# One ring of eight PSUM banks, decoding by masks, and a first pooling on TensorE, in a kernel ordered by a planner

## The chip, the core and the metric

The program runs on one core of a Trainium2 chip. The metric is the device time of one execution in microseconds (us); lower is better. TensorE multiplies, VectorE, ScalarE and GpSimd work element by element, SyncE issues the transfers, and PSUM is the memory into which TensorE writes (eight banks of 128 partitions x 512 fp32). In the profile the engines are PE (PEld for its weight loads), DVE, ACT, POOL and SP.

## What is computed

Three layers follow one another. An attention over eight batches of eight heads, 576 tokens and 64 channels, whose keys and values are first averaged over groups of eight tokens; then a mixture of four causal attention experts, of which the gate takes two for each token; then a layer that mixes tokens and channels with cosine and sine.

```python
def _attn_ref(q, k, v):                      # q, k, v: (8, 8, 576, 64)
    k_p = k.reshape(B, H, 72, 8, D).mean(axis=3)
    v_p = v.reshape(B, H, 72, 8, D).mean(axis=3)
    attn = softmax(q @ k_p.transpose(0, 1, 3, 2) / sqrt(D))
    return attn @ v_p

def _moe_ref(x, w_gate, wq, wk, wv, wo):     # x: (8, 576, 512), 4 experts of 64 channels, 2 taken
    ...
    a = softmax(causal(x @ wq[e] @ (x @ wk[e]).T / sqrt(64)))
    ye = a @ (x @ wv[e]) @ wo[e]
    ...

def _moe2_ref(x, w_theta, w_tok_r, w_tok_i, w_ch):
    theta = x @ w_theta
    y = w_tok_r @ (x * cos(theta)) + w_tok_i @ (x * sin(theta))
    u = x + y
    return u + maximum(u @ w_ch, 0)
```

Some weights of the third layer (w_theta, w_tok, w_ch) come as 64-bit numbers and are turned into fp32 on the chip: this is the decoding.

## The kernel before

**Precision.** Nearly every product is made of three: each factor is held as a high half, rounded to the engine's short fp32 format, and a low half, the rest (`mm3`, line 481). The usual way out of PSUM is thus a pair: ScalarE copies (and so rounds) the product into the high half, VectorE subtracts that half from the product and writes the low one.

**Two halves.** The first half makes attention and experts. For each batch `pool_kv` (line 713) averages keys and values by adding, on GpSimd (for the first batch partly on VectorE, `FIRST_DVE`, line 28). ScalarE copies the pooled keys into `kbd`, the values into `vbd`; each is a block matrix whose zero half was cleared at the start, so both are written by halves of 64 partitions. `attn_half` (line 754) makes scores for tiles of 128 queries; `WHOLE` (line 26) says for which tiles the exponentials are made in one instruction (VectorE subtracts the maximum and sums) and for which in eight, one for each head with its own sum (ScalarE). It then transposes the scores (`pm`, `pq`) and multiplies by the values. `proj_qk` (815) and `proj_v` (847) make the experts' queries, keys, values and gates; the keys (`kh`) are copied to the other half of the partitions by a transfer. `scores`, `norm`, `turn` and `heads` (902 to 962) do the experts' attention. Attention of batch b+1 is interleaved with the experts of batch b, and `decode` (672) runs in four blocks for each of the first six batches; its results go to DRAM (`thD`, `tokD`) and are read back for the second half. The second half is `mix` (1105: angles, sine, cosine, times x) and `tokens` (1155: the two big products and the output).

**Banks.** Products of the projections, values, experts' outputs and the second half's big products take one of two banks called `acc`, transposes one of two called `t`, scores and the mixing's products one of four called `s`.

**Order.** The order of instructions on each engine is written out before the kernel is built. `Plan` (197) collects every instruction with what it depends on. `part` and `arrange` (332, 341) give each a key, a wished-for time: the start of its part in `PARTS` (43), spread over the part's length, plus a `SHIFT` (58) for its engine and the tensor that it writes. `issue` (361) then runs a list of engines with estimated durations (`price`, 305) and takes, at each step, the instruction that can start first, ties by key. Line 466 is where all instructions are issued, so every row of the profile names that line; tensors tell them apart.

Of the kernel before, what the change touches and what calls it, by code (L numbers as in the profile page):

```python
# [25 lines left out]
WHOLE = {1, 2, 3, 4}, {0}  # L26

FIRST_DVE = {"k0", "k2", "pm0", "v0", "vr", "vrb0", "w0", "w3", "w4", "w6"}
# [15 lines left out]
    "first": (-1302.83, 63.19), "kv first": (-249.24, 366.9), "attn first 0": (-2208.92, 30.55),  # L44
    "attn first 1": (-552.72, 6.54), "proj_v first 0": (-1145.19, 56.03), "proj_qk0 first 0": (-185.37, 1302.94),
# [3 lines left out]
    "moe1": (29.54, 22.32), "decode": (150.23, 0.58), "wp": (-141.08, 3.51), "loadc first": (-6.04, 1083.14),  # L49
    "wtok first": (-212.16, 3987.86), "moe1 last": (27.48, 103.73), "mix first": (770.4, 161.1),  # L50
    "wtok": (2281.89, 4299.31), "wch": (-794.95, 122.81), "loadc": (-901.73, 22508671.56), "tokens": (85.02, 33.36),
    "mix": (85.18, 31.94), "constants first": (-1492.94, 5143.97), "clear first": (-2169.17, 8594480.35),
    "weights first": (-1120.91, 244.57), "load 1": (-21.92, 2656.27), "load first k": (-1565.62, 16.63),
    "load first q": (-1211.16, 0.84), "load first v": (-1596.57, 239.37),
}
SHIFT = {
    "ACT.G": 310.7, "ACT.G*": -60.8, "ACT.chs": 547.28, "ACT.d_hi": 469.68, "ACT.d_raw": -47.45, "ACT.d_s": 807.39,
    "ACT.gates": 299.94, "ACT.gates*": 299.58, "ACT.kbd": -11.49, "ACT.kbd*": -340.09, "ACT.kh": -2.28,
    "ACT.kh*": 65.35, "ACT.pa": -42.54, "ACT.pa*": 44.32, "ACT.pev": 4.6, "ACT.pev*": -912.36, "ACT.pod": -26.03,
    "ACT.pod*": 798.55, "ACT.pp": 2.9, "ACT.pp*": -1318.06, "ACT.pr": -176.41, "ACT.pr*": -24.35, "ACT.pt": -169.18,  # L60
    "ACT.pt*": -352.19, "ACT.qs": -10.6, "ACT.qs*": -463.58, "ACT.r": -71.52, "ACT.r*": 9.14, "ACT.th": 625.3,
    "ACT.th*": -370.35, "ACT.us": 161.03, "ACT.v": -127.44, "ACT.v*": 190.03, "ACT.vbd": -58.15, "ACT.vbd*": -1060.98,
    "ACT.vrh": 239.89, "ACT.vrh*": 411.06, "ACT.wT": 282.39, "ACT.warm": -205.54, "ACT.wos": -220.19,
    "ACT.wps": -74.18, "ACT.wqs*": -160.07, "ACT.wvs*": -767.36, "ACT.x": -165.21, "ACT.x*": -338.71,
    "ACT.xT": -426.63, "ACT.xT*": -238.01, "ACT.xt": 269.77, "ACT.xt*": -447.57, "ACT.yg": -290.43, "ACT.yg*": -78.87,
    "ACT.ys": -37.1, "ACT.ys*": 255.73, "ACT.yst": -83.9, "ACT.yst*": 34.37, "ACT.z": 76.22, "ACT.z*": -67.57,
    "ACT.zt": -607.59, "ACT.zt*": -849.31, "CTL.": 608.37, "DMA.": -426.39, "DMA.d_raw": 513.05, "DMA.kh": 303.04,
    "DMA.kh*": 585.01, "DMA.kraw": 171.92, "DMA.kraw*": 98.53, "DMA.pev*": 255.52, "DMA.pm*": 185.77,
    "DMA.pod*": -63.81, "DMA.qraw": -231.98, "DMA.qraw*": -71.33, "DMA.thD": 250.39, "DMA.ths": 592.41,
    "DMA.tokD": 134.39, "DMA.toks": -521.25, "DMA.toks*": -394.74, "DMA.v": -569.25, "DMA.v*": 95.2,  # L70
    "DMA.vraw": 149.85, "DMA.vraw*": -103.2, "DMA.vrem": 318.96, "DMA.vrem*": 108.24, "DMA.x": 69.1,
    "DMA.ygD": -74.78, "DMA.ygD*": -418.7, "DMA.yraw": 159.13, "DMA.yraw*": -144.65, "DMA.ytail": -390.7,
    "DMA.ytail*": 114.16, "DMA.zf": 736.52, "DVE.before*": 163.28, "DVE.cmp": -602.52, "DVE.cmp*": -395.89,
    "DVE.d_raw": 67.78, "DVE.flush": 65.65, "DVE.gates*": -533.48, "DVE.hm*": 633.13, "DVE.hpi": 704.94,
    "DVE.ident": -188.3, "DVE.kl": -3.31, "DVE.kl*": -148.18, "DVE.kt*": -647.74, "DVE.l": -309.76, "DVE.l*": 24.84,
    "DVE.lb": -7.23, "DVE.lb*": -163.3, "DVE.limit*": 210.65, "DVE.logit": 221.32, "DVE.logit*": 367.23,
    "DVE.m": -56.69, "DVE.m*": -115.98, "DVE.mask*": 659.33, "DVE.mx": 144.89, "DVE.mx*": 334.45, "DVE.o": -41.03,
# [14 lines left out]
    "POOL.vbd*": -610.85, "POOL.vrb": -61.96, "POOL.vrb*": 327.56, "POOL.vrl": -106.84, "POOL.vt": -45.14,  # L92
    "POOL.vt*": 491.07, "POOL.wT": 171.13, "POOL.wos": 289.44, "POOL.wqs*": -1583.79, "POOL.wvs*": 204.79,
    "POOL.yraw": 435.28, "POOL.yraw*": 343.16, "POOL.ys": -841.0, "POOL.ys*": -50.81, "POOL.yst": 441.93,
    "POOL.yst*": -91.42, "POOL.ytail": 463.31, "POOL.ytail*": 436.57, "POOL.z": 255.2, "POOL.z*": -199.85,
}


# [1164 lines left out]
```

## Time and profile before

| | us |
|---|---|
| median of 3 runs (980.51 to 984.83) | 982.76 |
| the profiled execution's own time | 980.56 |
| its span, first to last instruction | 978.8 |
| TensorE busy | 916.0 (94%) |
| ScalarE busy | 650.3 (66%) |
| VectorE busy | 600.0 (61%) |
| GpSimd busy | 516.7 (53%) |

The 1.8 us between span and time lie around the program. The shares are means over two very different halves, so they are read by stretches of the span. A product's busy time runs until it has drained, some 0.28 us for one that takes 0.12 us in a row of others, so a busy TensorE isn't one at its peak.

### The profile page before, as it was taken

Reading aid. Unit: us, or ns where it says so; the run is one execution under the profiler, and the core shown is the slowest. Engines: PE = TensorE matmul, PEld = TensorE weight load, DVE = VectorE, ACT = ScalarE, POOL = GpSimd, SP = SyncE. Lnnn points to the kernel's source line nnn. Section 1 sums busy time; section 2 is a strip of 40 time slices with the busy share of each in tenths; the row PEclk is TensorE's granted clock in tenths of the full one; section 3 lists DMA queues with packets and bytes.
Section 4 is the critical chain, followed back from the end, with each engine's and each line's share of the span. In section 5 each row is a group of like instructions: output and inputs, shape, how many; then the busy total and the mean of one; then the engine's idle time right before and its main releaser. Section 6 shows DMA issues by size and latency. Waiting matters only on the chain.

```text
span 978.8 us, 19095 instructions
## 1 busy us (share of the span) xinstructions
PE 916.0 (94%) x6384; PEld 858.5 (88%) x6384; DVE 600.0 (61%) x1718; ACT 650.3 (66%) x2026; POOL 516.7 (53%) x693
## 2 busy tenths in 40 slices
PE   2888999999899999999888999999999999999998
PEld 2887988898889899988866799999999999999998
DVE  5877887787878788887756745272424534262412
ACT  4689989798888999987768864262535444363510
POOL 7877777577386755544355774261625335151420
PEclk9999999999999999999989999999999999999999
DMA  9444445335444433334277413020110202010001
GB/s 279 138 143 122 122 123 150 115 108 140 119 118 116 136 96 87 89 103 115 51 232 243 154 44 92 1 85 13 38 56 13 80 1 70 1 38 13 25 25 49
DMA packets 78434, 91.63 MB, mean 94 GB/s; under 512 B 11264, under 2 KB 60928, under 8 KB 78336
## 3 DMA queue, kind: packets, MB, share of 16 engines
q1 hardware_dynamic: 78336, 90.41, 31.4%
q8 instruction: 51, 0.84, 0.4%
q14 instruction: 47, 0.39, 0.1%
HBM read 58.34 MB, written 26.28 MB: 86 GB/s over the span
## 4 chain that ended last, share of the span: by engine, by line
PE 64%; ACT 17%; DVE 8%; DMA 4%; POOL 3%; issue 3%; SPq 1%; POOLq 0%; ACTq 0%; DVEq 0%
PE acc L466 46%; PE s L466 14%; PE t L466 4%; ACT pp L466 4%; ACT pt L466 2%; DMA kh<-kh 2%; ACT pev L466 2%; ACT qs L466 1%; DVE s L466 1%; ACT kh L466 1%; ACT pa L466 1%; DVE pa L466 1%; DMA qraw<-in_qT_dram 1%; ACT xT L466 1%; DVE kl L466 1%
## 5 line engine op out<-in xcount | busy, mean ns | idle before, releaser
L466 PE MATMUL acc<-toks,z 128*128 128x288 f32 x1536 | 242.3, 297 | 2.0 <-ACT z L466 1.0
L466 PEld LDWEIGHTS acc<-toks,z 128*128 128x128 f32 x1536 | 223.9, 188 | 9.5 <-POOL z L466 1.8
L466 POOL TENSOR_TENSOR us<-u,us 128x288 fp32r<-128x288 f32 x64 | 51.9, 811 | 198.4 <-ACT us L466 198.3
L466 PE MATMUL acc<-xT,wqs 128*128 128x256 f32 (+1 forms) x768 | 123.3, 303 | 3.4 <-DVE logit L466 1.4
L466 PE MATMUL acc<-us,chs 128*128 128x288 f32 x768 | 114.1, 297 | 0.6 <-DVE o L466 0.5
L466 PEld LDWEIGHTS acc<-xT,wqs 128*128 128x128 f32 x768 | 106.4, 189 | 7.5 <-PE acc L466 3.4
L466 PEld LDWEIGHTS acc<-us,chs 128*128 128x128 f32 x768 | 107.9, 188 | 5.0 <-DVE o L466 1.5
L466 DVE TENSOR_TENSOR u<-acc,xt 128x288 f32<-128x288 f32 x64 | 29.1, 455 | 132.4 <-PE acc L466 132.4
L466 ACT CAST us<-u 128x288 fp32r<-128x288 f32 x64 | 27.6, 431 | 120.6 <-DVE u L466 120.5
L466 POOL TENSOR_TENSOR z<-zf,z 128x512 fp32r<-128x512 f32 x64 | 81.9, 1298 | 33.7 <-ACT z L466 33.6
L466 POOL TENSOR_SCALAR pev<-pev,lb,G 128x128 f32<-128x128 f32 (+4 forms) x80 | 52.5, 657 | 72.6 <-DVE lb L466 30.0
L466 DVE TENSOR_TENSOR pt<-t,pt 128x512 fp32r<-128x512 f32 (+4 forms) x160 | 75.7, 484 | 15.2 <-ACT pt L466 13.2
L466 ACT ACTIVATE pp<-s,mx 128x72 f32<-128x72 f32 x232 | 74.6, 336 | 6.6 <-DVE mx L466 6.0
L466 PE MATMUL acc<-wvs,xT 128*128 128x260 f32 x480 | 77.6, 292 | 1.2 <-DVE kl L466 0.4
L466 DVE CUSTOM_DVE_ANT_0 s<-s,mask 128x128 f32<-128x128 f32 (+2 forms) x144 | 69.6, 494 | 14.7 <-PE s L466 12.7
L466 ACT CAST pt<-t 128x512 fp32r<-128x512 f32 (+4 forms) x160 | 67.8, 437 | 13.8 <-PE t L466 12.9
L466 PE MATMUL s<-kbd,qraw 128*128 128x144 f32 x320 | 60.3, 311 | 16.2 <-DMA qraw<-in_qT_dram 12.3
L466 PE MATMUL acc<-pt,v 128*128 128x320 f32 (+4 forms) x416 | 68.1, 296 | 5.6 <-ACT yg L466 1.6
L466 PE MATMUL s<-kh,qs 128*128 128x128 f32 (+2 forms) x192 | 62.3, 355 | 10.3 <-DMA kh<-kh 8.0
L466 PEld LDWEIGHTS acc<-pt,v 128*128 128x128 f32 x416 | 60.7, 191 | 11.2 <-ACT yg L466 3.1
L466 PEld LDWEIGHTS acc<-wvs,xT 128*128 128x128 f32 x480 | 65.5, 189 | 4.0 <-ACT yg L466 0.8
L466 PE MATMUL s<-wos,ys 128*128 128x512 f32 x192 | 66.1, 402 | 0.4 <-DVE zf L466 0.3
(177 smaller groups left out, 2244.8 us busy)
## 6 DMA issues: line engine op xcount, KB each, us to landing
qraw<-in_qT_dram SPq DMA_DIRECT2D x40, 256.0 KB, 3.6
out_dram<-o SPq DMA_DIRECT2D x64, 144.0 KB, 1.8
kraw<-in_kT_dram SPq DMA_DIRECT2D x15, 576.0 KB, 4.1
yraw<-ygD SPq DMA_DIRECT2D x16, 512.0 KB, 4.3
vraw<-in_vm_dram SPq DMA_DIRECT2D x15, 512.0 KB, 4.1
d_raw<-in_wtok_dram SPq DMA_DIRECT2D x18, 288.0 KB, 2.9
toks<-tokD SPq DMA_DIRECT2D x18, 288.0 KB, 6.0
ygD<-yg SPq DMA_DIRECT2D x32, 160.0 KB, 2.9
```

What stands on the lines that cost most here:

```text
L466: o.ins = o.fn(*[a.real() if isinstance(a, View) else a for a in o.args], **{k: a.real() if isinstance(a, View) else a for k, a in o.kw.it ...
```

## The change

It does the following:

- All products take a bank of one ring of eight (`bank()`), in place of the three rings.
- `decode` makes the sign and magnitude with masks on VectorE: three ScalarE instructions go, VectorE has four in place of two. High and low halves lie in one tile and go to DRAM in one transfer.
- For the first batch keys and values are summed by TensorE, eight products with the identity into one bank, and taken out by VectorE (keys) or by ScalarE and VectorE (values). For the others the pooled sums are spread over the block matrix by one multiplication with a mask (`half64`, `half`) over all 128 partitions; the clearing of `kbd` and `vbd` goes. The values of the last eight groups (`vr`) have their high and low half in the two halves of one tile, and so do the scores that meet them.
- Tile 2 of the batches after the first is made whole. In the mixing the rounding constant is added by ScalarE out of PSUM and taken off by VectorE; for the first batch VectorE makes the absolute value.
- The planner has new keys, keys by kind of product on TensorE, separate parts for the last attention batch (`_z`) and the first mixing (`_a`), a price of 118 ns where an instruction's starting partitions differ from those of the one before on its engine, and longer transfers (1700 for 1300 ns, and 1.7 times the bytes between places of the SBUF).

```diff
-WHOLE = {1, 2, 3, 4}, {0}
-FIRST_DVE = {"k0", "k2", "pm0", "v0", "vr", "vrb0", "w0", "w3", "w4", "w6"}
+WHOLE = {1, 2, 3, 4}, {0, 2}
+FIRST_DVE = {"pm0"}
...
-        o.kind = eng + "." + (outs[0].root.name.rstrip("0123456789") if outs else "")
+        o.kind = "PE." + self.lane if eng == "PE" else eng + "." + (outs[0].root.name.rstrip("0123456789") if outs else "")
...
+        if eng == "DMA" and all(isinstance(a, View) and not a.root.pool.dram for a in args[:2]):
+            o.bytes *= 1.7
...
+    TURN = 118.0
-    DMA_ISSUE, DMA_LAT, DMA_RATE, DMA_ALL, DMA_SLOT, RELEASE = 600.0, 1300.0, 184.0, 262.0, 150.0, 130.0
+    DMA_ISSUE, DMA_LAT, DMA_RATE, DMA_ALL, DMA_SLOT, RELEASE = 600.0, 1700.0, 184.0, 262.0, 150.0, 130.0
...
-                t = free[e]
                 for o in cs:
+                    t = free[e] + (self.TURN if o.base != base[e] else 0.0)
...
+    def bank():
+        return ps.tile([128, 512], F32, name="s", bufs=8)
...
-    P.memset(kbd, 0.0)
-    for t in vbd:
-        P.memset(f(t), 0.0)
...
+    for t, x in ((half, 1.0), (half64, 1.0 / 64)):
+        V.memset(t, 0.0)
+        for e in range(2):
+            V.memset(t[64 * e:64 * e + 64, e:e + 1], x)
...
-        A.activation(s, hi_w.bitcast(F32), AF.Copy, bias=FLUSH)
-        V.tensor_scalar(t, hi_w, 3, 0x40000000, op0=OP.logical_shift_left, op1=OP.bitwise_xor)
+        V.tensor_scalar(s, hi_w.bitcast(F32), FLUSH, FLUSH, op0=OP.add, op1=OP.not_equal)
+        V.tensor_scalar(t, hi_w, 3, 0x3FFFFFFF, op0=OP.logical_shift_left, op1=OP.bitwise_and)
         V.scalar_tensor_tensor(t, lo_w, 29, t, op0=OP.logical_shift_right, op1=OP.bitwise_or)
-        A.activation(s, s, AF.Sign, bias=flush)
-        A.activation(t.bitcast(F32), t.bitcast(F32), AF.Abs)
+        V.scalar_tensor_tensor(t, hi_w, -0x40000000, t, op0=OP.bitwise_and, op1=OP.bitwise_or)
         P.tensor_tensor(s, s, t.bitcast(F32), op=OP.mult)
         A.copy(hi, s)
         P.tensor_tensor(lo, s, f(hi), op=OP.subtract)
...
-        for d, p in zip(dst, parts):
-            D.dma_start(d, f(p))
+        D.dma_start(dst, f(decode(src, n, dec)))
...
+        def summed(raw, n, k):
+            pl.lane = "pool"
+            acc = bank()[:, :n * k]
+            for r in range(8):
+                T.matmul(acc, ident, raw[:, :, r], start=r == 0, stop=r == 7)
+            return acc.rearrange("d (p k) -> d p k", k=k)[:, :, None, :]
...
+            if b == 0:
+                V.tensor_tensor(kbd[:, p_], summed(raw, n, 72).to_broadcast([128, n, 2, 72]),
+                                half64[:, None, :, None].to_broadcast([128, n, 2, 72]), op=OP.mult)
+                continue
...
-            for e in range(2):
-                s_ = slice(64 * e, 64 * e + 64)
-                A.activation(kbd[s_, p:p + n, e], t[s_, :, 0], AF.Copy, scale=1.0 / 64)
+            X.tensor_tensor(kbd[:, p_], t[:, :, 0:1].to_broadcast([128, 2, 2, 72]),
+                            half64[:, None, :, None].to_broadcast([128, 2, 2, 72]), op=OP.mult)
...
+            if b == 0:
+                acc = summed(raw, n, 64)[:, :, 0]
+                for e in range(2):
+                    A.activation(vbd[0][:, p_, e], acc, AF.Copy, scale=half[:, e:e + 1])
+                for e in range(2):
+                    V.scalar_tensor_tensor(vbd[1][:, p_, e], acc, half[:, e:e + 1], f(vbd[0][:, p_, e]),
+                                           op0=OP.mult, op1=OP.subtract)
+                continue
...
-            for e in range(2):
-                s_ = slice(64 * e, 64 * e + 64)
-                A.copy(vbd[0][s_, p:p + n, e], t[s_, :, 0])
-                X.tensor_tensor(vbd[1][s_, p:p + n, e], t[s_, :, 0], f(vbd[0][s_, p:p + n, e]), op=OP.subtract)
+            X.tensor_tensor(t[:, :, 2:4], t[:, :, 0:1].to_broadcast([128, 2, 2, 64]),
+                            half[:, None, :, None].to_broadcast([128, 2, 2, 64]), op=OP.mult)
+            A.copy(vbd[0][:, p_], t[:, :, 2:4])
+            X.tensor_tensor(vbd[1][:, p_], t[:, :, 2:4], f(vbd[0][:, p_]), op=OP.subtract)
...
-                s_ = ps.tile([128, 512], F32, name="s", bufs=4)[:, :288]
+                s_ = bank()[:, :288]
...
-            acc = ps.tile([128, 512], F32, name="acc")
+            acc = bank()
...
-            V.tensor_scalar(th[:m], pth[:m], INV2PI, MAGIC, op0=OP.mult, op1=OP.add)
-            A.activation(th[:m], th[:m], AF.Copy, bias=-MAGIC)
+            A.activation(th[:m], pth[:m], AF.Copy, bias=MAGIC, scale=INV2PI)
+            V.tensor_scalar(th[:m], th[:m], -MAGIC, None, op0=OP.add)
...
-            A.activation(th[:m], r[:m], AF.Abs)
+            if b == 0:
+                V.tensor_scalar(th[:m].bitcast(I32), r[:m].bitcast(I32), 0x7FFFFFFF, None, op0=OP.bitwise_and)
+            else:
+                A.activation(th[:m], r[:m], AF.Abs)
```

## Rows read from the trace of the kernel before

**Rows 1.** Stretches: length, busy us (count) PE, PEld, DVE, ACT, POOL; clock, DMA, GB/s.

```profile
0.00:57.50 57.50, 35.76 (x239) 32.94 (x240) 40.29 (x134) 34.01 (x117) 46.10 (x85) 1.00 0.67 204
57.50:415.10 357.60, 335.60 (x2447) 314.32 (x2447) 288.27 (x991) 319.88 (x1266) 239.01 (x374) 0.99 0.42 118
357.80:415.10 57.30, 55.92 (x417) 52.72 (x417) 49.06 (x170) 54.12 (x213) 32.62 (x51) 1.00 0.35 95
415.10:500.00 84.90, 76.60 (x545) 70.15 (x544) 63.93 (x226) 66.71 (x210) 34.63 (x59) 1.00 0.37 101
500.00:552.00 52.00, 44.87 (x211) 35.17 (x212) 32.64 (x64) 42.64 (x89) 32.66 (x29) 0.94 0.74 235
525.00:550.00 25.00, 20.01 (x93) 14.00 (x91) 17.29 (x29) 24.18 (x48) 15.74 (x14) 1.00 0.61 208
552.00:978.80 426.80, 423.19 (x2947) 405.92 (x2946) 174.82 (x305) 187.05 (x350) 164.33 (x149) 1.00 0.13 40
```

**Rows 2.** Waits of VectorE from 57.5 to 415.1 us (total, times, longest).

```profile
DVE xT L466 <- ACT xT L466: 9.5, 16, 2.5
...
DVE pr L466 <- ACT pr L466: 1.9, 5, 0.9
```

**Rows 3.** Decoding on ScalarE, groups of instructions (busy, mean ns, idle before).

```profile
L466 ACT ACTIVATE d_s<-d_s,flush 128x288 f32<-128x288 f32 (+1 forms) x34 | 18.0, 528 | 0.5
...
L466 ACT ACTIVATE d_raw<-d_raw 128x288 f32<-128x288 f32 (+1 forms) x34 | 15.7, 463 | 3.7 <-DVE d_raw L466 3.4
L466 ACT ACTIVATE d_s<-d_raw 128x288 f32<-128x288 f32 (+1 forms) x34 | 15.7, 463 | 5.7 <-DMA d_raw<-in_wch_dram 3.0 <-DMA d_raw<-in_wtok_dram 1.3 <-DMA d_raw<-in_wth_dram 0.8
```

**Rows 4.** Decoding on VectorE, instructions of one tile (min/median/max ns, first and last).

```profile
L466 DVE TENSOR_SCALAR d_raw<-d_raw x34: 254/310/2429, 43.2 to 588.4; 128x288 int32<-128x288 int32 x18, 128x256 int32<-128x256 int32 x16
L466 DVE SCALAR_TENSOR_TENSOR d_raw<-d_raw x34: 407/450/1034, 43.8 to 590.8; 128x288 int32<-128x288 int32 x18, 128x256 int32<-128x256 int32 x16
```

**Rows 5.** Chain of waits: four heads' exponentials and sums (start, us, what).

```profile
14.11 1.32 ACT pp L466 x8
```

**Rows 6.** Groups of instructions: whole tiles, pooled keys and values, a GpSimd product.

```profile
L466 POOL TENSOR_TENSOR d_s<-d_s,d_raw 128x288 f32<-128x288 f32 (+1 forms) x34 | 27.0, 795 | 35.6 <-ACT d_raw L466 25.5 <-DVE lb L466 3.6 <-issue 2.9
...
L466 ACT ACTIVATE kbd<-kt 64x144 f32<-64x144 f32 (+1 forms) x34 | 10.7, 316 | 3.1 <-DVE kt L466 1.6 <-POOL kt L466 0.9 <-PE s L466 0.3
...
L466 ACT CAST vbd<-vt 64x128 fp32r<-64x128 f32 (+1 forms) x34 | 9.9, 290 | 5.2 <-DVE vt L466 4.5 <-POOL vt L466 0.3
...
L466 DVE TENSOR_TENSOR pp<-s,mx 128x288 f32<-128x288 f32 x22 | 9.4, 451 | 0.2
...
L466 DVE TENSOR_REDUCE l<-pp 128x8 f32<-128x584 f32 x11 | 8.3, 753 | 1.6 <-ACT pp L466 1.6
...
L466 ACT ACTIVATE pp<-pp 128x576 f32<-128x576 f32 x11 | 7.5, 683 | 3.8 <-DVE pp L466 3.6 <-ACT wqs L466 0.2
```

**Rows 7.** Waits of TensorE from 57.5 to 415.1 us.

```profile
PE s L466 <- DMA kh<-kh: 5.6, 6, 2.1
PE acc L466 <- DVE logit L466: 2.3, 7, 1.1
```

**Rows 8.** TensorE's first products in order of time (start, us, what, idle before).

```profile
12.28 1.78 PE L466 MATMUL s<-kbd,qraw 128*128 128x144 f32 x6 [12.28 <-DMA qraw<-in_qT_dram]
17.05 2.77 PE L466 MATMUL s<-kbd,qraw 128*128 128x144 f32 x10 [2.99 <-ACT kbd L466]
22.27 1.12 PE L466 MATMUL t<-ident,pm 128*128 128x128 f32 x4 [2.45 <-DVE pm L466]
...
27.25 0.66 PE L466 MATMUL s<-kbd,qraw 128*128 128x144 f32 x4
```

**Rows 9.** Groups of ScalarE's instructions from 500 to 552 us.

```profile
L466 ACT ACTIVATE th<-r 128x512 f32<-128x512 f32 x5 | 3.2, 637 | 0.1
```

**Rows 10.** Groups of instructions: two subtractions of VectorE in the start.

```profile
L466 DVE TENSOR_TENSOR wvs<-pev,wvs 128x260 fp32r<-128x260 f32 x1 | 1.0, 1043 | 0.0
...
L466 DVE TENSOR_TENSOR wvs<-pod,wvs 128x260 fp32r<-128x260 f32 x1 | 0.4, 430 | 1.8 <-ACT wvs L466 1.8
```

More of the change, by code (lines that the diff above doesn't have):

```diff
@@ L59 @@
[L59 to L63, printed above, removed]
@@ L69 @@
[L69 to L73, printed above, removed]
@@ L758, in attn_half @@
         pa = [awork.tile([128, 4, 320], F32R, name=f"pa{c}", bufs=1) for c in range(2)]
-        pr = awork.tile([128, 320], F32R, name="pr", bufs=1)
+        pr = [awork.tile([128, 320], F32R, name=f"pr{c}", bufs=1) for c in range(2)]
         for o, new in tiles:
@@ L820, in proj_qk @@
             for w in range(2):
-                acc = ps.tile([128, 512], F32, name="acc")
+                acc = bank()
                 c0 = 256 * p + 128 * w
@@ L854, in proj_v @@
             h, o = (0, 128 * t) if t < 2 else (1, min(128 * t, S - 128) - 256)
-            acc = ps.tile([128, 512], F32, name="acc")
+            acc = bank()
             for kt in range(4):
@@ L915, in scores @@
         for c0, m in parts:
-            a = ps.tile([128, 512], F32, name="s", bufs=4)[:, :m]
+            a = bank()[:, :m]
             last = c0 + m == n
@@ L943, in turn @@
         nj = min(i // 2 + 1, 4)
-        t = ps.tile([128, 4, 128], F32, name="t")
+        t = bank().rearrange("p (k q) -> p k q", k=4)
         for j in range(nj):
@@ L955, in turn @@
         if i == 8:
-            t = ps.tile([128, 4, 128], F32, name="t")
+            t = bank().rearrange("p (k q) -> p k q", k=4)
             T.transpose(t[:, 0], pb[:, 448:576], ident)
@@ L968, in heads @@
         for e in range(2):
-            acc = ps.tile([128, 512], F32, name="acc")
+            acc = bank()
             nj = 2 if h == 0 else 4
@@ L1063, in body @@
         for c in range(2):
-            D.dma_start(f(th_s[c][:, k]), thD[c][k])
+            D.dma_start(f(th_s[c][:, k]), thD[k][:, c])
     pl.lane = "wp"
     for m in range(2):
-        acc = ps.tile([128, 512], F32, name="acc")
+        acc = bank()
         for k in range(4):
@@ L1114, in mix @@
             m = tok.stop - tok.start
[L1115 to L1116 removed]
+            px = bank()
+            pth = bank()
             for k in range(2):
@@ L1145, in mix @@
             pl.lane = "mixt"
-            pt = ps.tile([128, 4, 128], F32, name="t")
+            pt = bank().rearrange("p (k q) -> p k q", k=4)
             for d in range(4):
@@ L1162, in tokens @@
                 tk = slice(288 * h, 288 * h + 288)
-                py = ps.tile([128, 512], F32, name="acc")[:, :288]
+                py = bank()[:, :288]
                 for k in range(9):
@@ L1173, in tokens @@
                 o = cz.tile([128, 288], F32, name="o")
-                ph = ps.tile([128, 512], F32, name="acc")[:, :288]
+                ph = bank()[:, :288]
                 for k in range(4):
```

195 lines of the change are left out of this document (105 added, 90 removed), and 7 rows, old and new, of the table PARTS.

## The prediction, made before the result was known

> **What bounds the kernel now.** I read the windows first, cut at events of the program: up to 57.5 us is the start (the first batch's value projection ends there), 57.5 to 415.1 us holds six cycles in which attention of one batch runs beside the experts of the batch before it, 415.1 to 500 us the last expert work without attention, 500 to 552 us the change to the second half, and from 552 us on come the token products [rows 1]. In the second half TensorE is busy 423.19 of 426.80 us; nothing of this change shortens its products, so I leave that half alone. The gain must come from the first 552 us.
>
> There a cycle lasts 357.60 / 6 = 59.6 us. Per cycle, from the same row: TensorE 55.9 us busy, ScalarE 53.3, VectorE 48.0, GpSimd 39.8. TensorE's busy time is flattered, since a short burst counts until its last product has drained; the next view says who it waits for. I take the waits of VectorE in this stretch: nine of its eleven rows, 9.5 down to 1.9 us and 47.5 us together, name ScalarE [rows 2]. The pattern is one of the code: ScalarE rounds a product into its high half, and VectorE subtracts that half to get the low one. So ScalarE, at 53.3 of 59.6 us (89.4%), paces VectorE, and both pace TensorE's banks. In the best cycle ScalarE reaches 54.12 of 57.30 us, 94.4% [rows 1]. It is the bound of these cycles, with TensorE close behind.
>
> **Decode by masks.** Each block loses three ScalarE instructions (the added constant, the sign, the absolute value): 463 + 528 + 463 ns [rows 3], 1.45 us, four blocks a cycle: ScalarE -5.8 us. VectorE gains one instruction with one tensor operand and one with two; their medians now are 310 and 450 ns [rows 4], so +0.76 us each, +3.0 us a cycle. GpSimd keeps its two. The two stores of a block become one, one issue less on SyncE's queue; nobody waits for it, so nothing.
>
> **Tile 2 done whole.** For batches after the first, one more of five query tiles takes its exponentials in one instruction. ScalarE loses two groups of 1.32 us [rows 5] and gains one of 683 ns [rows 6]: -2.0 us. VectorE gains two subtractions of 451 ns and a long sum of 753 ns [rows 6]; the short sum that goes I leave out: +1.7 us.
>
> **Pooled keys and values after the first batch.** ScalarE's four key copies (316 ns) and four value copies (290 ns) [rows 6] become two value copies of twice the size; each costs between one and two of the old ones, 290 to 580 ns, and I take 430, since part of 290 is not per element: -1.6 us. GpSimd gains multiplications and loses narrow subtractions; at 795 ns for 128x288 [rows 6] the two key products cost 1.6 us, and the rest I bound by 0 and 2 us: +2.6 us on 39.8. It idles 20 us a cycle, so I cost that at nothing; if the pooled keys come to be waited for, it costs up to those 2.6 us a cycle.
>
> So ScalarE goes from 53.3 to 53.3 - 5.8 - 2.0 - 1.6 = 43.9 us a cycle and VectorE from 48.0 to 48.0 + 3.0 + 1.7 = 52.7 us. **The bound passes to VectorE**, but one that no longer waits for ScalarE as often. What share can it reach? ScalarE reached 89.4% on average and 94.4% at best; I take the middle, 91.9%: 52.7 / 0.919 = 57.3 us, 2.3 us less than now. TensorE's 55.9 us busy fit into that (in the best cycle it has 55.92 of 57.30). Ends: 52.7 / 0.894 = 58.9 us and TensorE's own 55.9 us. Six cycles: **-14 us** (-4 to -22).
>
> **One ring of eight banks and the new keys.** Now "acc" has two banks, "t" two, "s" four. A product takes the next free bank of all; the added wait, if a bank is read late, stands on TensorE, whose queue is in order, so all products behind it wait. The waits that name a reader of "acc" (VectorE's logits) are 2.3 us in six cycles, those for the copy of keys between partition halves 5.6 us [rows 7]. Together 1.3 us a cycle. The reordering may give this or lose it; it lies inside the bounds above and I add nothing for it.
>
> **Start.** TensorE begins at 12.28 us, when the first query tile lands, then waits 2.99 us for ScalarE's copy of pooled keys and 2.45 us for VectorE's normalised scores [rows 8]. The key and value pooling becomes 96 product instructions on TensorE: 32 of 128 or 144 columns and 64 of half that. Bounds: at the slow pace below, 32 x 0.24 + 64 x 0.12 = 15 us, at the fast one half of it. TensorE is idle for 12.28 us and half of the next 12, which covers most of it; where it doesn't, it costs up to 4 us. The two waits are 5.4 us, of which I take 4. There is a second effect. The ten products from 17.05 us take 2.77 us, about 0.25 each, while four of the same from 27.25 us take 0.66, about 0.13 after the drain of the last [rows 8]: before the first ones TensorE had been idle, and up to 25 us its products run at half the later pace, 1.2 against 2.4 GHz. (The granted clock of that stretch reads 1.00 [rows 1], so the pace is read off the products.) Some 30 instructions at half pace cost 3.5 us; products from about 5 us on may raise the pace sooner, and I take half: -1.7. Start: **-5.7 us** (+4 to -9).
>
> The Trainium skill (TensorE: Matmul & The Clock Gate, Part 1) says that the throttled clock is the default and that activity releases it. By it the pooling would pay for the warming and the whole 3.5 us would come back, 1.8 us more than in my sum; a colder reading would leave it at zero.
>
> **415 to 500 us.** No attention runs here and only two blocks are decoded; TensorE idles 8.3 of 84.9 us [rows 1]. I take **-1.5 us** (0 to -4). **500 to 552 us.** TensorE idles 7.1 us, 5 of them between 525 and 550 us, where ScalarE is busy 24.18 of 25 us [rows 1]. ScalarE loses the first mixing's five absolute values, 3.2 us in all, and six decode instructions of 0.46 to 0.53 us [rows 3, 9]. That is 6 us of its work; next late is VectorE, busy 17.29 of 25, or GpSimd. I take **-4 us** (0 to -7).
>
> Sum: -14 - 5.7 - 1.5 - 4 = -25.2 us on the profiled execution's 980.56 us, 955.4 us. That execution lies 2.2 us below the median of the runs shown, 982.76, so the forecast is **957.6 us**. The rivals' times stand on the median, too.
>
> **Rivals.** *TensorE is reached*: waits shrink until the cycle is TensorE's 55.9 us, 6 x -3.7 = -22, and the start gives 9, 415 to 500 us 4 and the change of halves 7: -42, 941 us. For it: VectorE's waits for ScalarE are 47.5 us in six cycles, far more than it needs. Against: 52.7 / 55.9 is 94%, ScalarE's best.
>
> *VectorE takes ScalarE's place at its average share*: 58.9 us a cycle, -4; start -3, change of halves -3: -10, 973 us.
>
> *Slower: VectorE's new work collides with GpSimd.* The masks bring four instructions a cycle with two operands in the ordinary memory. Of two like subtractions in the start one took 430 ns and one 1043, while GpSimd was running [rows 10]; a collision thus costs 0.61 us. If all four new ones meet it, VectorE's work is 52.7 + 2.4 = 55.1 us, at ScalarE's average share 61.6 us a cycle, +2.0 x 6 = +12 us, and with -3 from the start and nothing elsewhere the kernel takes 992 us. It decides from where the six cycles lose more than the rest gives (3 us, so 60.1 us a cycle, VectorE's work over 53.7 us): two of the four. Against it: the present two-operand instruction has a median of 450 ns and a maximum of 1034 over 34 [rows 4], so collisions are the exception now.
>
> The Trainium skill (SBUF — State Buffer, Who interferes with whom) states this as a rule: a VectorE instruction with two such operands contends with a GpSimd instruction that reads there, while ScalarE never waits for another engine. It speaks against taking the decode off ScalarE; the rows agree that the collision exists and show it rarely.
>
> *It doesn't do what it says*: the order gives back what ScalarE saves, 979 to 985 us.
>
> **How the numbers follow.** Chances: forecast (946 to 966 us) 0.50, TensorE reached 0.20, average share 0.13, collision 0.10, no change 0.07. The range runs from under the first rival, 934 us, to 978 us, and leaves the collision and most of "no change" out. This kernel's measurement tells 0.5% from no change, 4.9 us; faster by more is 0.50 + 0.20 + 0.13 = 0.83, same 0.07, slower 0.10.
>
> **What would show it.** Right: in the six cycles ScalarE near 44 us and VectorE near 53 us of 57, VectorE's waits for ScalarE down by half, the first products near 5 us, the wait for pooled keys gone, the second half still some 427 us. Wrong: VectorE's two-operand decode instructions at 0.8 us or more, or a VectorE share well under 89% with TensorE waiting for banks that VectorE has still to read; or a second half that grows, which I have counted at nothing.

## The result, and the profile after

The changed kernel takes **953.76 us** (median, 952.24 to 955.62) beside 981.63 us of the kernel before on the same chip: a ratio of 0.9714, 95% interval 0.968 to 0.9748, some 28 us faster. The forecast was 957.6 us with a range of 934 to 978. The profiled execution took 952.24 us with a span of 950.5 us, where [rows 1] come from a span of 978.8 us. One execution below, the profiled one of the changed program with three rings and keys fitted to it, ran slow, at a granted clock of 0.654 (1290.98 us), so that the median given for this program is of its other three and no trace of it is read.

The page's line of busy times, of the kernel after (busy us, share of the span, instructions):

```profile
PE 912.6 (96%) x6480; PEld 871.5 (92%) x6480; DVE 610.4 (64%) x1798; ACT 576.8 (61%) x1758; POOL 526.9 (55%) x683
```

ScalarE has lost 73.5 us of its 650.3, VectorE has gained 10.4 and GpSimd 10.2. TensorE has 96 product instructions more (the pooling).

Windows of the kernel after, cut at the same events as [rows 1]: the end of the first batch's value projection, of the seventh's, and of the last expert's output (columns as in [rows 1]: length, busy time and instructions of each engine, granted clock, transfers):

```profile
0.00:53.70 53.70, 45.89 (x335) 45.19 (x336) 34.76 (x130) 27.45 (x98) 37.16 (x63) 0.94 0.68 205
53.70:394.90 341.20, 327.18 (x2449) 314.12 (x2448) 300.92 (x1040) 275.43 (x1064) 256.47 (x386) 0.98 0.44 124
394.90:501.10 106.20, 98.90 (x671) 91.26 (x670) 81.81 (x281) 76.42 (x232) 55.02 (x75) 0.97 0.52 153
...
501.10:555.50 54.40, 49.96 (x316) 45.75 (x316) 37.96 (x70) 35.28 (x70) 34.97 (x31) 0.97 0.47 149
555.50:946.90 391.40, 390.69 (x2719) 375.13 (x2717) 154.51 (x281) 162.20 (x299) 143.30 (x130) 1.00 0.11 35
```

And the windows of the kernel before that answer to the last three:

```profile
415.10:520.60 105.50, 95.31 (x640) 86.45 (x640) 75.58 (x257) 79.03 (x239) 50.08 (x72) 0.97 0.48 139
...
520.60:581.10 60.50, 55.26 (x332) 47.50 (x332) 34.49 (x60) 49.44 (x99) 35.47 (x36) 1.00 0.42 134
581.10:975.70 394.60, 394.04 (x2733) 377.28 (x2732) 160.86 (x278) 167.93 (x309) 146.07 (x129) 1.00 0.12 37
```

The start goes from 57.5 to 53.7 us (-3.8), the six cycles from 357.6 to 341.2 (-16.4), what lies between them and the first of the last big products from 166.0 to 160.6 (-5.4), the rest from 397.7 to 395.0 (-2.7): -28.3 us, the difference of the spans. More than half of it lies in the six cycles, as forecast.

What VectorE and then TensorE wait for in the six cycles of the kernel after (us in total, times, longest), beside [rows 2] and [rows 7]:

```profile
DVE l L487 <- ACT pp L487: 6.5, 11, 1.1
DVE xT L487 <- ACT xT L487: 5.3, 11, 0.8
DVE pt L487 <- ACT pt L487: 4.4, 13, 1.1
DVE v L487 <- ACT v L487: 4.2, 11, 0.9
...
DVE qs L487 <- ACT qs L487: 2.6, 6, 0.7
```

```profile
PE s L487 <- POOL pev L487: 3.9, 3, 3.2
PE s L487 <- POOL pm L487: 3.4, 2, 1.8
PE s L487 <- POOL kbd L487: 3.2, 2, 2.9
PE s L487 <- DVE pt L487: 1.0, 3, 0.5
```

VectorE's waits for ScalarE, over all rows of the view, have come down from 48.2 to 26.3 us. TensorE no longer waits for the transfer of keys or for a logit; what is late for it now is above all GpSimd, 10.5 us in the first seven waits of this list.

### The profile page after: what moved, and what is told of

Read it like the earlier page. It is cut to its first block, busy times and chain, and to the rows that moved or that the text cites. A ratio compares the mean times of both kernels' runs of the same rounds, so it can differ in the third digit from the quotient of the medians.

```text
span 950.5 us, 19095 instructions
## 1 busy us (share of the span) xinstructions
PE 912.6 (96%) x6480; PEld 871.5 (92%) x6480; DVE 610.4 (64%) x1798; ACT 576.8 (61%) x1758; POOL 526.9 (55%) x683
## 4 chain that ended last, share of the span: by engine, by line
PE 83%; DVE 7%; ACT 4%; POOL 3%; issue 2%; DMA 1%; POOLq 0%; ACTq 0%; DVEq 0%
PE s L487 83%; DVE pt L487 1%; DVE s L487 1%; DVE d_t L487 1%; DVE th L487 1%; ACT pt L487 1%; POOL kv L487 1%; ACT pp L487 1%; ACT th L487 1%; DVE mx L487 1%; POOL z L487 0%; DMA kraw<-in_kT_dram 0%; DVE pa L487 0%; DVE pp L487 0%; ACT pev L487 0%
## 5 line engine op out<-in xcount | busy, mean ns | idle before, releaser
L487 PE MATMUL s<-toks,z 128*128 128x288 f32 x1536 | 217.2, 295 | 0.0
L487 PEld LDWEIGHTS s<-toks,z 128*128 128x128 f32 x1536 | 208.8, 188 | 0.9
L487 PE MATMUL s<-xT,wqs 128*128 128x256 f32 (+1 forms) x768 | 118.6, 299 | 0.0
L487 PE MATMUL s<-us,chs 128*128 128x288 f32 x768 | 111.8, 296 | 0.2 <-POOL chs L487 0.2
L487 PEld LDWEIGHTS s<-us,chs 128*128 128x128 f32 x768 | 107.1, 188 | 4.1 <-ACT chs L487 0.4
L487 PEld LDWEIGHTS s<-xT,wqs 128*128 128x128 f32 x768 | 104.3, 188 | 0.4
L487 DVE TENSOR_TENSOR pt<-s,pt 128x512 fp32r<-128x512 f32 (+4 forms) x160 | 74.9, 485 | 10.8 <-ACT pt L487 9.2
L487 ACT CAST pt<-s 128x512 fp32r<-128x512 f32 (+4 forms) x160 | 65.8, 433 | 23.3 <-PE s L487 22.5
L487 PE MATMUL s<-wvs,xT 128*128 128x260 f32 x480 | 75.3, 294 | 0.0
L487 PE MATMUL s<-pt,v 128*128 128x320 f32 (+4 forms) x416 | 67.6, 294 | 2.3 <-DVE pt L487 0.8
L487 ACT CAST z<-zf 128x512 fp32r<-128x512 f32 x64 | 39.5, 622 | 48.2 <-DVE zf L487 26.9
L487 PEld LDWEIGHTS s<-pt,v 128*128 128x128 f32 x416 | 60.5, 190 | 6.4 <-DVE pt L487 2.2
L487 ACT ACTIVATE pp<-s,mx 128x72 f32<-128x72 f32 x176 | 56.1, 345 | 10.4 <-DVE mx L487 6.1
```

What stands on the lines that cost most here:

```text
L487: o.ins = o.fn(*[a.real() if isinstance(a, View) else a for a in o.args], **{k: a.real() if isinstance(a, View) else a for k, a in o.kw.it ...
```

## The experiments

Two theories stood first. **Work**: the gain is ScalarE's shorter work, as the prediction argued. **Order**: each engine runs its instructions in the order that the keys fixed, so the gain is the new order, and the engines' loads count for little. After eight runs the second was split again, and the last four runs ask what in the program lets the new order be so short.

### ScalarE's work taken away, the order kept

The three ScalarE instructions of the kernel before's decode are not issued; all others keep their place. The kernel thus leaves out a part of the decoding.

```diff
-        A.activation(s, hi_w.bitcast(F32), AF.Copy, bias=FLUSH)
+        pl.skip.add(A.activation(s, hi_w.bitcast(F32), AF.Copy, bias=FLUSH))
...
         for o in order:
+            if o in self.skip:
+                continue
```

> The kernel before with its order of instructions kept as it is, but without the three ScalarE instructions of each decoded block (the decoded weights lose their sign handling by this: that part of the computation is left out). VectorE's and TensorE's work is as before; ScalarE has 1.45 us less at each of 34 blocks, 26 of them in the first half. Work theory (ScalarE's load paced the cycles, and its relief is what the change gains): 12 to 20 us faster than before, 962 to 970. Order theory (the gain comes from the new keys and the ring; ScalarE's work was hidden): at most 4 us faster.

975.52 us beside 978.33, ratio 0.9961 (0.9941 to 0.9982): **3.8 us** for 38.8 us less of ScalarE's work (650.3 to 611.5 us busy). The windows show the six cycles of this run:

```profile
57.20:410.60 353.40, 333.12 (x2448) 312.40 (x2447) 287.61 (x991) 300.95 (x1213) 236.96 (x375) 1.00 0.42 119
```

A cycle has 50.2 us of ScalarE's work in place of 53.3 [rows 1] and takes 58.9 us in place of 59.6. By the prediction's rule (ScalarE paces VectorE) it should have given most of the 14 us. The work theory falls as it stood: with the order kept, ScalarE's relief gives little.

### Work added to each engine, the order kept

In the changed kernel, 26 decoded blocks (all but `chs`) bring with them three ScalarE copies, or three VectorE instructions with two operands, or two GpSimd sums, all of 128x288 on tiles that nothing else uses.

```diff
         for o in order:
+            if o in self.extra:
+                self.more()
...
+        for _ in range(3):
+            nc.scalar.activation(spare[2].real(), spare[0].real(), AF.Copy)
```

> The changed kernel with its order kept and three spare ScalarE copies of 128x288 (about 1.4 us together) put ahead of the rounding of each of the 26 blocks decoded in the first half: ScalarE's work of decoding as in the kernel before, VectorE's new work kept. Work theory: ScalarE's share of a cycle goes from 81% to near 90%, and some 26 x 0.3 to 0.5 us come back: 8 to 14 us slower than the changed kernel, 962 to 968. Order theory: ScalarE has room for it, at most 4 us.

> The changed kernel with its order kept and three spare two-operand VectorE instructions of 128x288 (about 1.35 us together) at each of the 26 blocks decoded in the first half. If VectorE has become the bound, as I forecast: nearly each added microsecond shows, 20 to 35 us slower than the changed kernel. If TensorE's order and GpSimd's late results hold the cycles, VectorE having 6 us of room in each: 5 to 12 us.

> The changed kernel with its order kept and two spare GpSimd additions of 128x288 (about 1.6 us together) at each of the 26 blocks decoded in the first half. If GpSimd has become the one that TensorE waits for (its pev, pm and kbd are the three longest waits of TensorE in the cycles, 10.5 us): 12 to 25 us slower than the changed kernel. If VectorE is the bound and GpSimd has 14 us of room in each cycle: at most 8 us.

| added to | busy added, us | median | ratio to before | over the changed kernel |
|---|---|---|---|---|
| ScalarE | 29.4 | 975.83 | 0.9966 (0.9944 to 0.9988) | 22 to 25 us |
| VectorE | 49.3 | 994.78 | 1.0169 (1.0137 to 1.0201) | 41 to 45 us |
| GpSimd | 41.1 | 976.92 | 0.9979 (0.9961 to 0.9998) | 23 to 26 us |

The last column has the difference of the medians and that of the ratios, of 980 us. With the order kept, added work costs 0.75, 0.83 and 0.56 us or a little more for each busy us, whatever the engine; work taken away from the kernel before gave 0.1. ScalarE's 22 to 25 us miss the order theory's 4 as well as the work theory's 8 to 14; VectorE's lie above both of its ranges, and only GpSimd's touch the upper one of theirs. So no single engine is the bound of this order. My reading is that a fixed order passes a delay on from wherever it arises, while an earlier end is of use only if everything else that the next step needs is early as well. By it the slower runs are the price of work that an order wasn't made for, and don't restore the work theory. The run further down that gives ScalarE its old decode back in an order fitted to it bears this out: it costs 2.8 us in place of 22 (though VectorE loses its two new instructions there).

The two-operand VectorE instructions that were added tell of the collision rival. One line for the added ones (min/median/max ns, first and last start), one for those of the changed kernel's own decode:

```profile
L692 DVE SCALAR_TENSOR_TENSOR spare<-spare,spare x78: 432/586/1210, 41.4 to 490.5; 128x288 int32<-128x288 int32 x78
```

```profile
L487 DVE SCALAR_TENSOR_TENSOR d_t<-d_raw,d_t x68: 407/448/1235, 20.2 to 570.0; 128x288 int32<-128x288 int32 x36, 128x256 int32<-128x256 int32 x32
```

The kernel's own 68 keep the median of [rows 4], 448 against 450 ns, the longest 1235. The added ones, which the order knows nothing of, have a median of 586, and VectorE's busy time grew by 49.3 us where 78 x 0.45 make 35. Taken one by one in the trace, the 24 that started while GpSimd ran nothing took at most 461 ns; the 54 that started while a GpSimd instruction was running have a median of 800. Of the changed kernel's own, 47 started beside an idle GpSimd and took at most 460 ns, the other 21 have a median of 551. In the kernel before it was 10 of 34 that started beside a running one, so the masks made such meetings no more frequent.

### One set of keys on the other program

> The changed kernel's instructions, ring and planner model, but planned with the keys of the kernel before (the changed kernel's new tensors, which have no old key, at shift 0; the parts for the last batch and the first mixing fall back on the general ones). Order theory: most of the gain goes, 970 to 985. Work theory: most of it stays, 955 to 965, since the planner can use the freed ScalarE with any sensible keys.

> The kernel before with its instructions, its three rings and its planner model, planned with the changed kernel's keys (renamed where a tensor has another name; kinds that only the old kernel has keep their old keys). Order theory: much of the gain is there without the new instructions, 955 to 968. Work theory: no gain, and keys made for other instructions may cost, 978 to 1000.

The edits swap `PARTS` and `SHIFT`; names that only one program has take the key of the nearest of the other.

```diff
             kind, cycle, at = o.part
+            kind = kind.removesuffix("_z").removesuffix("_a")
             start, length = PARTS[kind]
```

The changed program with the old keys takes 987.07 us, ratio 1.0088 (1.0059 to 1.0118); the program before with the new keys 1035.18 us, 1.0586 (1.0544 to 1.0628). Neither number fits either theory: the new program without its keys is slower than before, and the keys without their program are far slower. (Of the second's 55 us more than before, 38 lie ahead of the first batch's value projection, which ends at 95.7 us in place of 57.5.) What TensorE waits for in the second, from 55 to 430 us:

```profile
PE acc L520 <- DVE qs L520: 9.6, 11, 1.7
PE acc L520 <- DVE xT L520: 6.5, 10, 1.0
PE acc L520 <- DVE kl L520: 3.7, 8, 0.8
PE acc L520 <- ACT yg L520: 2.8, 4, 1.0
PE acc L520 <- DVE logit L520: 2.6, 5, 1.3
```

```profile
L520 PE MATMUL s<-kh,qs x134: 221/322/628, 87.2 to 429.9; 128*128 128x288 f32 x44, 128*128 128x128 f32 x24, 128*128 128x256 f32 x22, 128*128 128x384 f32 x22
...
L520 DVE SCALAR_TENSOR_TENSOR qs<-acc,qs x59: 225/425/488, 83.1 to 430.0; 64x256 fp32r<-64x256 f32 x36, 64x320 fp32r<-64x320 f32 x12, 64x64 fp32r<-64x64 f32 x11
```

```profile
62.57 0.62 PE L520 MATMUL acc<-pa,vbd 128*128 128x256 f32 x3 [0.93 <-DVE xT L520]
```

```profile
L520 DVE SCALAR_TENSOR_TENSOR xT<-acc,xT x48: 410/432/492, 59.3 to 388.9; 128x256 fp32r<-128x256 f32 x24, 128x320 fp32r<-128x320 f32 x24
```

The `qs` rows say what kind of wait "acc <- DVE qs" is. The products that take `qs` as data write to "s"; VectorE's `qs` reads "acc". A product that writes "acc" and waits for it is waiting for the bank. `kl`, `yg` and `logit` are such waits too, 18.7 us in all with `qs`. The kernel before has 4.6 us for the same four in its six cycles, 2.3 of them for `logit` [rows 7]. Most of the waits for `xT` belong to them, too, as the last two rows show: seven of the ten stand before products of `pa` and `vbd`, which don't read `xT`, while VectorE's `xT` reads "acc". So the new order runs into the two banks of "acc".

### One part alone, planned with the keys at hand

The masks alone in the program before, with its keys, and the changed program with three rings, with its keys:

```diff
-        A.activation(s, s, AF.Sign, bias=flush)
-        A.activation(t.bitcast(F32), t.bitcast(F32), AF.Abs)
+        V.scalar_tensor_tensor(t, hi_w, -0x40000000, t, op0=OP.bitwise_and, op1=OP.bitwise_or)
```

> The kernel before with the decode by masks alone, planned again with the old keys (an old key that fits is kept, the new intermediate tile has shift 0). Work theory: ScalarE relieved by 5.8 us in a cycle and the planner free to use it: 8 to 16 us faster than before, 963 to 971. Order theory: within 4 us of before, either way.

```diff
-        return ps.tile([128, 512], F32, name="s", bufs=8)
+        return ps.tile([128, 512], F32, name=kind, bufs={"s": 4, "t": 2, "acc": 2}[kind])
```

> The changed kernel with three rings of banks again (four for scores and mixing products, two for transposes, two for the rest), planned again with the new keys. If the one ring carries much of the gain: 12 to 25 us slower than the changed kernel, with TensorE waiting for VectorE and ScalarE to read acc. If it carries only what the waits of before show (0.7 us a cycle): 3 to 6 us slower.

995.89 us, ratio 1.018 (1.0143 to 1.0217), and 1051.71 us, 1.0741 (1.07 to 1.0783). The masks alone are 18 us slower than before, though they take 38.1 us off ScalarE; neither theory had expected such a loss. The three rings cost 98 us, far over the 12 to 25 that were expected. The second run differs from the changed kernel in nothing but the rings and the order planned for them. Its six cycles, and TensorE's longest waits in them:

```profile
68.30:463.00 394.70, 342.86 (x2416) 324.51 (x2416) 317.11 (x1044) 276.87 (x1045) 261.38 (x389) 0.95 0.40 114
```

```profile
PE acc L487 <- DVE qs L487: 14.8, 11, 3.0
PE acc L487 <- DVE kl L487: 9.8, 7, 3.6
PE acc L487 <- DVE xT L487: 4.1, 7, 1.0
PE acc L487 <- DVE logit L487: 3.9, 4, 1.8
...
PE acc L487 <- ACT yg L487: 2.9, 5, 0.9
```

The cycles take 394.70 us in place of 341.20, and TensorE idles 51.8 us of them in place of 14.0; 31.4 us of that are waits for readers of "acc", without `xT`. So the new keys need the one ring. Both runs share a flaw, though: `issue` plans a new order, with keys that were fitted to another program, so they can't tell a bad part from bad keys. That these keys fail in three rings doesn't say that others would.

### Each program with keys fitted to it

To take that flaw away, four programs got keys from one and the same search: the changed planner, random moves of the keys, of the same length for each. The programs with one ring start from the new keys, those with three from the old. What separates two runs with the same start is then the program, as far as such a search goes; between one ring and three it is the start as well.

```diff
-CYCLE = 55.68
+CYCLE = 53.487077
```

(and so all of `PARTS` and `SHIFT`). The second run has the old decode as well, the third the three rings of the diff above, the fourth is the program before.

> The changed program, nothing left out, with its order keys fitted once more by a random search of a fixed length that moves the keys and keeps what lowers the planner's own end. It is the control of the next three, whose keys are fitted by the same search and length. If the changed kernel's keys are near what such a search can reach, 948 to 957 us; if the search fits the planner's picture and not the chip, 960 to 985.

> The changed program with one ring of eight banks, the TensorE pooling and the planner as changed, but the decode as before, with three ScalarE and two VectorE instructions ahead of the multiply; keys fitted anew by the same search as the control. Decode theory (the gain is ScalarE's relief): 965 to 980 us, 10 to 20 over the control, since ScalarE gets back some 8 us of work per cycle. Ring theory (the gain is that any product may take any free bank, which lets a fitted order run): within 5 us of the control, 948 to 960.

> The changed program with the masks and the TensorE pooling, but PSUM in three rings of 4, 2 and 2 banks by the kind of product as before; keys fitted anew by the same search as the control. Ring theory: 970 to 990 us, 15 to 35 over the control. Decode theory: within 6 us of the control, 950 to 962.

> The program of before (three rings, decode on ScalarE, pooling on VectorE and GpSimd) with the changed planner (its new costs, kinds and parts) and keys fitted anew by the same search as the control. If the new planner and a search are the gain, 950 to 965 us; if the program is, 975 to 1000, and by the ring theory it lies within 12 us of the run with three rings in the changed program.

| program | median | ratio to before |
|---|---|---|
| changed | 953.43 | 0.9736 (0.9711 to 0.9761) |
| changed, decode on ScalarE as before | 956.18 | 0.9758 (0.9732 to 0.9785) |
| changed, three rings | 991.35 | 1.011 (1.0072 to 1.0147) |
| before | 1003.15 | 1.0225 (1.0184 to 1.0265) |

The control stays where the changed kernel was: the search finds nothing better there and spoils nothing. **Putting the decode back on ScalarE costs 2.8 us**, and the two intervals overlap. The decode theory, and with it the work theory, is refuted. The ring theory is met by the old decode; with three rings both runs come out 1 to 3 us above its ranges, so in its direction and by more.

**The program with three rings takes 37 us more** than the control (1.011 - 0.9736, of 980). That is not the ring's price by itself, since the start of the search differs, too: no program with one ring was searched from the old keys. Two numbers say that this counts. The changed program with one ring and the old keys, not searched at all, took 987.07 us (1.0088), hardly less than the one with three rings after its search (1.011). And the program before comes out at 1003 us, slower than with its own keys (980), so this search from the old keys falls short by some 23 us there. The 37 us are thus the ring and the keys that go with it, together.

The two programs with three rings had the same start. Between them lies all of the change but the ring (masks, pooling, tile 2, pooled keys and values): 1.0225 - 1.011, some 11 us. If the search falls equally short in both, some 17 of the change's 28 us are left for the ring with its keys. That is an estimate. The granted clock doesn't separate the four programs: the executions at 0.989 to 0.991 took 952.46 to 953.89 us (control), 953.73 (old decode), 987.06 (three rings) and 997.88 (before).

Windows of the stretch that holds the six cycles: with the old decode in one ring, of the control, and of the program before with fitted keys:

```profile
51.30:390.90 339.60, 326.37 (x2455) 311.34 (x2454) 300.32 (x1013) 298.62 (x1137) 262.11 (x394) 0.99 0.47 134
```

```profile
51.50:383.20 331.70, 319.42 (x2403) 304.89 (x2402) 298.02 (x1018) 266.78 (x1021) 252.38 (x380) 0.99 0.45 128
```

```profile
65.90:438.00 372.10, 333.65 (x2394) 314.14 (x2393) 295.39 (x986) 316.08 (x1229) 246.35 (x381) 0.97 0.43 123
```

With the old decode ScalarE works 298.62 / 6 = 49.8 us a cycle, 3.9 more than in the changed kernel, and the cycle takes 339.60 / 6 = 56.6 us against 56.9 there. (In the control it is 55.3, but with 52 products of TensorE fewer in the stretch: 331.70 / 2403 and 339.60 / 2455 are both 0.138 us a product.) ScalarE's load doesn't set it. Nor does it set VectorE's waits for ScalarE: with this greater load they are 20.4 us over the stretch, less than the changed kernel's 26.3 and near the control's 18.7. The largest of them:

```profile
DVE xT L500 <- ACT xT L500: 4.6, 15, 1.1
DVE l L500 <- ACT pp L500: 3.4, 8, 0.9
```

In the program before with fitted keys TensorE meets the rings again. The rows of the tile `kl` from 55 to 385 us:

```profile
L549 DVE TENSOR_TENSOR kl<-acc,kh x40: 406/450/495, 55.1 to 384.0; 64x256 fp32r<-64x256 f32 x20, 64x320 fp32r<-64x320 f32 x20
...
  PE acc L549: 7.2, 8
```

VectorE's `kl` reads "acc", and the next products of "acc" wait 7.2 us for it, in eight places.

## Why the prediction was right, and where it was not

**The time was right, the reason for most of it was not.** The step that failed is the first one: from VectorE's waits, which name ScalarE [rows 2], and ScalarE's share of 89.4%, I concluded that ScalarE paces the cycles. Two runs speak against it: with the order kept, 39 us of its work less gave 3.8 us, and with an order fitted to it the old decode in the changed program loses 2.8 us. (The masks alone lost 18 us, but with keys that weren't theirs.) ScalarE's share after is 275.43 / 341.20 = 81%, VectorE's 88%, both under the 89.4% that I had taken for a pace. That the time came out within 4 us is luck as far as the decode goes: with the old decode the program takes 956.18 us, which lies in the middle of the forecast as well. A list of waits says who came last in this order; it doesn't say that the order would be shorter if that engine had less to do.

**The ring and the keys at nothing** was the second failed step, and the larger one: I looked for bank waits in the trace of before, found 2.3 us for `logit` [rows 7], and set the ring to zero. But the order of before had been made for three rings. I take it that it went around their waits, so that its rows show what it could not avoid, not what it gave up. What the runs show is that the new keys can't do without the ring (18.7 us of bank waits with them in the program before, 31.4 in the changed program with three rings, which loses 98 us), and that the ring with keys made for it is worth up to 37 us, by the estimate above some 17. The Trainium skill (Perfetto Trace Analysis, Matmul Optimizations) asks that all eight PSUM banks be used so that more instructions can run side by side. The kernel before used all eight as well, in rings of 4, 2 and 2, so no run here tests that sentence; the runs vary how the eight are handed out.

**The terms of the cycle.** In us per cycle, forecast and measured:

| | before | forecast | after | old decode, one ring |
|---|---|---|---|---|
| cycle | 59.6 | 57.3 | 56.9 | 56.6 |
| ScalarE | 53.3 | 43.9 | 45.9 | 49.8 |
| VectorE | 48.0 | 52.7 | 50.2 | 50.1 |
| GpSimd | 39.8 | 42.4 | 42.7 | 43.7 |

ScalarE's term was too large because I counted four blocks in a cycle. In the six cycles there are 17 (19 before), the others lie in the start and behind; three blocks make 53.3 - 4.4 - 2.0 - 1.6 = 45.3. The first of these rows shows the count, and that GpSimd waits for VectorE's masks; the second is GpSimd's new key product, which the text had at 0.8 us:

```profile
L487 POOL TENSOR_TENSOR d_s<-d_s,d_t 128x288 f32<-128x288 f32 (+1 forms) x17 | 13.3, 782 | 25.6 <-DVE d_t L487 14.7 <-DVE lb L487 10.3 <-DVE d_s L487 0.6
...
L487 POOL TENSOR_TENSOR kbd<-kv,half 128x288 f32<-128x288 f32 x12 | 8.1, 676 | 1.9 <-PE s L487 1.4
```

VectorE's term was +4.7 and is +2.1. With three blocks it is 2.3 + 1.7 = 4.0; the rest is that the durations of neighbours overlap. Added up, VectorE's durations in the six cycles grow from 339.0 to 364.3 us, 4.2 a cycle, while its busy time grows by 2.1. The cycle of 57.3 us came within 0.4 us by a share (91.9%) that VectorE never reached, of a load that it never had: two errors against each other.

GpSimd's 2.6 us were put at nothing, with the price named if pooled keys came to be waited for. They did: 3.2 us in two waits, and GpSimd is now the engine that TensorE waits for.

**Start: -5.7 forecast, -3.8 measured.** TensorE's rows in order of time, beside [rows 8]:

```profile
4.69 4.18 PE L487 MATMUL s<-kraw,ident 128*128 128x144 f32 x16 [4.69 <-DMA kraw<-in_kT_dram]
8.66 4.33 PE L487 MATMUL s<-pev,ident 128*128 128x72 f32 x32
12.82 1.55 PE L487 MATMUL s<-vraw,ident 128*128 128x128 f32 x12
14.21 2.13 PE L487 MATMUL s<-kbd,qraw 128*128 128x144 f32 x16
16.17 0.61 PE L487 MATMUL s<-vraw,ident 128*128 128x128 f32 x4
16.62 3.68 PE L487 MATMUL s<-pm,ident 128*128 128x64 f32 x32
...
24.08 0.36 PE L487 MATMUL s<-pa,vbd 128*128 128x256 f32 x1 [0.19 <-DVE pp L487]
24.27 1.07 PE L487 MATMUL s<-kbd,qraw 128*128 128x144 f32 x6
27.80 0.79 PE L487 MATMUL s<-pa,vbd 128*128 128x256 f32 x2 [2.46 <-DVE vbd L487]
```

The products begin near 5 us and the wait for the pooled keys is gone, as said. (Tiles that have given their place carry the next owner's name: the x32 are the pooling, too.) The first 60 pooling products run from 4.69 to 14.2 us, past the 12.28 us up to which TensorE had been idle, so the first scores start 1.9 us later than before: part of the bound's 4 us that I had not taken. Together the 96 take some 14 us, near my bound for the slow pace, though the last of them run at the fast one. The lower bound was wrong: the 32 products of 64 columns take 0.115 us each, hardly less than those of 128 columns (1.55 / 12 = 0.129), where I had taken half. The 2.46 us for VectorE's `vbd` are a new wait, where I had taken 4 of 5.4 us as won.

Sixteen score products take 2.13 us here, 0.13 each, where six and ten took 1.78 and 2.77 us [rows 8]: 2.4 us less, between the 1.7 that I took and the 3.5 at most. The first pooling products still take 0.26 us each for 144 columns, those from 12.82 us on 0.13 for 128; the engine had been idle until 4.69 us. The Trainium skill (TensorE: Matmul & The Clock Gate, Part 1) has the slow clock as the default, released by activity; the pace of these rows agrees, and the pooling pays for the warming in part. The -3.8 us are of one execution: with the same start, the run with VectorE's added work reached this cut at 51.2 us with a granted clock of 1.00, where this one took 53.7 with 0.94.

**Behind the cycles.** -1.5 and -4 were forecast up to the token products, -5.5; measured are -5.4. The split was wrong: to the end of the last expert the change is +0.7 (105.5 to 106.2), from there to the token products -6.1 (60.5 to 54.4), where ScalarE's work fell from 49.44 to 35.28 us. A part of both is products that changed sides: the first of these stretches has 31 more of them, worth some 4 us at 0.144 us each, the second 16 fewer. The second half, put at nothing, has the same pace: 394.60 / 2733 = 0.144 us a product before and 391.40 / 2719 = 0.144 after. Its 2.7 us are mostly 14 products that moved ahead of the cut.

**The rivals.** TensorE reached, 941 us: not so; it still idles 14 us in the six cycles. Its condition came nearest, since TensorE is busy 96% there, before 94%. VectorE at ScalarE's average share, 973 us: VectorE runs at 88%, under that share, and the kernel is still faster, so the share was no law. The collision, 992 us: the median of the kernel's own two-operand instructions didn't move. The Trainium skill (SBUF — State Buffer, Who interferes with whom) has two such operands contend with GpSimd's reads. The added VectorE instructions agree with it: they are long where a GpSimd instruction was already running, a median of 800 ns, and at most 461 where none was. Of the changed kernel's own, 21 of 68 met one, no larger a part than before, so the rival's condition, two of four, wasn't reached. No change, 979 to 985 us: not so.

**What stays open.** How the 28 us divide between the ring and its keys isn't known: the run that would tell, one ring with keys searched from the old ones, was not made. The old decode in one ring is 24 us faster than before and has, besides the ring, the pooling on TensorE, the wider tile 2 and the one multiplication for pooled keys and values; these were not run one by one. Before's own order with nothing changed but the bank of each product was not tried either, so it isn't known whether the ring gives anything without new keys. Nor was a longer search, which might find more for three rings.

## What to carry to other kernels

Where the order on every engine is fixed, a wait's name and an engine's share don't tell what a relief is worth: take the work away with the order kept, then compare the parts with the order fitted anew for each, from the same start, since all four programs planned here with another program's keys came out slower. An order that was made around a resource (banks, here) can show few waits for it in the trace; price the resource by planning without its limits, not by its waits alone. And count instructions in the stretch that is argued about, not by the loop that issues them.

## What the runs showed of the hardware

An instruction's price on VectorE hangs on what GpSimd does when it starts. A two-operand instruction of 128x288 or 128x256 that started beside an idle GpSimd took at most 461 ns, in the changed kernel and in the run with added ones; one that started while a GpSimd instruction was running took up to 1.2 us, with medians of 551 and 800 ns. Where GpSimd started second, the VectorE instruction kept its 0.45 us.

Among the pooling products, one of 64 columns on TensorE took 0.115 us at the fast pace, hardly less than one of 128 columns with 0.129.

In the run with VectorE's added work TensorE's granted clock is lower, too. Its start, its six cycles and the stretch behind them, cut at the same events as in the changed kernel above:

```profile
0.00:51.20 51.20, 42.83 (x335) 41.64 (x336) 35.78 (x131) 26.68 (x95) 36.82 (x62) 1.00 0.71 216
51.20:422.70 371.50, 339.42 (x2449) 321.65 (x2448) 332.50 (x1092) 277.65 (x1068) 264.12 (x386) 0.96 0.40 114
422.70:541.00 118.30, 103.18 (x672) 94.22 (x671) 95.85 (x307) 76.21 (x232) 55.79 (x75) 0.94 0.46 137
```

The cycles are 30.3 us longer, the stretch behind them 12.1. TensorE is busy 339.42 / 371.50 = 91% and 87% of them, against 96% and 93% in the changed kernel, and the clock is 0.96 and 0.94 against 0.98 and 0.97: a mean below 1 is time at the lower of its two levels (1.2 in place of 2.4 GHz). How much of those 41 to 45 us that is was not measured by itself. The busy share alone doesn't give the clock: the kernel before, busy 94% in its six cycles, has 0.99 [rows 1].
